# Attention plus MLP on one core: a step's block transposition moved ahead of the burst in program order, and the last turned exponential one step sooner

## The chip, the cores and the metric

The kernel runs on one core of one Trainium2 chip. The core has five engines that run their own instruction streams in order and meet through semaphores: TensorE (PE; its weight loads are shown as PEld), VectorE (DVE), ScalarE (ACT), GpSimd (POOL) and SyncE (SP, which here only issues DMAs). The metric is the device time of one execution in microseconds; lower is better.

## What is computed

An input of 2048 rows by 448 columns is normalised, and then runs through two branches whose results are added to the input: attention with 16 query heads of width 28 that share one key and one value head, and an MLP with 1792 hidden columns.

```python
xn = layernorm(x)
# branch A: 16 query heads, one key head, one value head, Dh = 28
q = (xn @ wq) as 16 heads;  k = xn @ wk;  v = xn @ wv
p = softmax(q k^T * Dh**-0.5);  A = (p v, heads side by side) @ wo
# branch B
h = gelu(layernorm(xn) @ w1 + b1);  B = h @ w2 + b2
out = x + A + B
```

## The kernel before

The first part of the kernel (to about 487 us of the span) projects q, k and v and runs the whole MLP. The rest is attention, which the change touches.

**Units and steps.** Attention is cut into 16 units `u`: four chunks of 512 query rows times four groups of four heads. A unit is worked off in 8 steps, each of two key tiles `kt`, `kt+1` of 128 keys: 128 steps `n`, step `n` being unit `n // 8`. "Position" below means `n % 8`, so `kt` = 2 x position.

**Ordinary heads.** For a pair of (key tile, head) jobs, `scores` takes a tile `p`, issues two matmuls into a PSUM tile `s` (L791) and one exponential on ACT (L793) that writes `p`, keys on partitions and queries along the free dimension. In the last eleven steps the third job of a step goes through two banks of the small PSUM pool `m` with two exponentials instead (L785, L786).

**Turned heads.** In units 2 to 15 the fourth head of the group goes another way, so that the row maximum is found on the way. `turned_scores` computes its scores with queries on partitions, four matmuls for 128 queries (L742), each evacuated by a DVE instruction that also gives a maximum (L743); these are the "t" pieces. `turned_exp` (the "x" piece) exponentiates half of such a tile on ACT (L760) and issues 8 DMAs, 5 on SP and 3 on POOL (L764), that lay it out in the tile `turned[u]` so that 32 x 32 blocks are all that is left to transpose. `turn_blocks` (the "T" piece) takes a tile `p` and transposes two key tiles' blocks from `turned[u]` into it with one DVE instruction (L769). A unit's turned scores and exponentials are made during the unit before it; its last exponential is issued at the last step of that unit, and its first transposition at its own first step, `kt` = 0.

**The burst.** The "P" piece pops two key tiles from a queue that lags by one step: the burst of step `n` multiplies with the values what step `n-1` produced, 8 multiplications for the accumulator `po` (L722; each leaves two records in the trace). Of each four, the first three read ordinary heads and the fourth reads the tile that T wrote.

**Other pieces.** "m" is one step of the stream that finds the row maxima of ordinary heads ahead of time (matmul L485, DVE reduction L486); it runs in most steps once or twice. "e" brings the maxima of the next unit into place, once a unit (L468 to L473). "o" is one output tile (12 matmuls L636 to L638, one DVE addition L640), when there is one. "n" moves the normalisation of the finished unit on (among others the reciprocal L666 on DVE, small DMAs and products on POOL). At `kt` = 0 `load_q` loads the queries of the next unit (L457, tile `xh`, issued on POOL).

**Order.** Nothing is scheduled: each engine runs its instructions in the order in which the Python program emits them. A string gives that order for a step, one letter a piece; for turned units it is the second one of

```python
ORDERS = ("mptmpmtmpmexnPpmonm", "ptmpeoxnPptmTn")
```

so a turned step is: p, t, m, p, e, o, x, n, burst, p, t, m, T, n. `jobs` starts with three jobs, one taken by each "p".

**Buffers.** Tiles `p` come from a ring of 7, four taken per step. `turned` has two tiles, `raw` (scores of the turned head) three. The PSUM pool `m` has three banks, shared by t, m, e, o and, at the end, the third p; `s` has two double banks and `po` one bank.

Of the kernel before, what the change touches and what calls it, by code (L numbers as in the profile page):

```python
# [24 lines left out]
SCALE = DH ** -0.5  # L25
BURST = 2
MLP_MAX = 20
ORDERS = ("mptmpmtmpmexnPpmonm", "ptmpeoxnPptmTn")
TURNED = tuple(range(2, 16))
RAWS = 3  # L30
LEAD = 11
# [5 lines left out]
def block_kernel(ctx, tc, x, wq, wk, wv, wo, w1, b1, w2, b2, out):  # L37
# [361 lines left out]
    NU = len(units)  # L399
# [16 lines left out]
    for c in range(NCH):  # L416
        center, turn = norm_parts((c + 1) % NCH, c + 1 == NCH)
        for i in range(4):
# [7 lines left out]
            if i in ((2, 3) if c == 0 else (1, 3)):  # L426
                n = 2 * c + i // 3
# [19 lines left out]
    def load_q(u):  # L447
        c, g = units[u]
        cols = slice(c * CW, (c + 1) * CW)
        if u < 2:  # L450
            qst.append(xt_p.tile([P, 4, CW], F32R, name="xh"))
            pool.memset(f(qst[u]), 0.0)
        qs = qst[u % 2]
        for blk, i in ((1, 0), (2, 0), (0, 1), (3, 1)):
            nh = heads_of(u)
            src = qd[i][4 * DH * g:4 * DH * g + DH * nh, cols].rearrange("(j r) n -> r j n", r=DH)
            loads.dma_start(f(qs[32 * blk:32 * blk + DH, 0:nh, :]), src)  # L457
        qss[u] = qs
# [5 lines left out]
    def load_max(u):  # L464
        qs, mr = qss[u], mrs.pop(u)
        nh = heads_of(u)
        pm = mtile([nh * CT, P])
        pe.transpose(pm, mr[:, 0:nh * CT], ident)  # L468
        mn = keep.tile([4 * CT, 2, P], F32R, name="mn", bufs=1)[0:nh * CT]
        act.activation(mn[:, 0, :], pm, AF.Copy, scale=-1.0)  # L470
        dve.scalar_tensor_tensor(mn[:, 1, :], pm, -1.0, f(mn[:, 0, :]), op0=ALU.mult, op1=ALU.subtract)
        loads.dma_start(f(qs[60:61, 0:nh, :]), f(mn[:, 0, :]))
        loads.dma_start(f(qs[124:125, 0:nh, :]), f(mn[:, 1, :]))  # L473
# [128 lines left out]
    def turned_tile():  # L602
        return att.tile([P, 4 * CT, CW], F32, name="turned", bufs=2)
# [14 lines left out]
    def prep_wo(g):  # L618
        act.activation(woh[:, g, :], wor[:, g, :], AF.Copy)
        pool.tensor_sub(wol[:, g, :], wor[:, g, :], f(woh[:, g, :]))  # L620
# [8 lines left out]
    def o_jobs(c, gs, tiles=range(CT)):  # L629
        last = NG - 1 in gs  # L630
        for k in tiles:
            po = mtile([P, D])
            ts = slice(k * P, (k + 1) * P)
            for g in gs:
                oth, otl = ots[c, g]
                pe.matmul(po, oth[:, ts], woh[:, g, :], start=(g == gs[0]), stop=False)  # L636
                pe.matmul(po, oth[:, ts], wol[:, g, :], start=False, stop=False)  # L637
                pe.matmul(po, otl[:, ts], woh[:, g, :], start=False, stop=(g == gs[-1]))  # L638
            a = rows[c, k]
            dve.tensor_add(a, a, po)  # L640
            if last:
                (nc.scalar if k % 2 and c == NCH - 1 else nc.sync).dma_start(ov[:, CT * c + k, :], a)
            yield
# [73 lines left out]
    def pv(u, kt):  # L717
        if kt == 0:
            pos[u] = op.tile([P, CW], F32, name="po")
        po = pos[u]  # L720
        for j in range(4):
            pe.matmul(po[32 * j:32 * j + 32, :], vs[:, kt, :], ps.pop((u, kt, j)),  # L722
                      start=(kt == 0), stop=(kt == NT - 1))
        if kt == NT - 1:
            if u == NU - 1:
                end_jobs(u, pos.pop(u))
                return
            side.add(norm_jobs(u, pos.pop(u)))
            side.step()
            c, g = units[u]  # L730
            if c < NCH - 1 and g == NG - 1:
                oside.add(o_wait(c, range(NG), range(CT)))
# [20 lines left out]
    def turned_exp():  # L753
        if not exps:
            return
        u, t, raw, m3, h = exps.pop(0)
        if u not in turned:
            turned[u] = turned_tile()
        rs = slice(2 * h, 2 * h + 2)
        act.activation(raw[:, rs], raw[:, rs], AF.Exp, bias=m3[:, 4:5], scale=1.0)  # L760
        for r in range(2 * h, 2 * h + 2):
            for a in range(4):
                q = pool if a == 3 or (a == 2 and r % 2) else nc.sync
                q.dma_start(turned[u][32 * r:32 * r + 32, 4 * t + a, :],  # L764
                            raw[32 * a:32 * a + 32, r].rearrange("p b i -> p (b i)"))

    def turn_blocks(u, kt):
        p = pair_of()
        dve.transpose(p.rearrange("p k (g j) -> p g k j", j=32),  # L769
                      turned[u][:, :, 32 * kt:32 * kt + 64].rearrange("p g (k j) -> p g k j", j=32))  # L770
        ps[u, kt, 3], ps[u, kt + 1, 3] = p[:, 0], p[:, 1]
# [8 lines left out]
    def scores(u, kt, jobs, apart):  # L780
        p = pair_of()
        if apart:
            for i, (k, j) in enumerate(jobs):
                s = mtile([P, CW])
                pe.matmul(s, ks[:, (kt + k) * P:(kt + k + 1) * P], qss[u][:, j, :], start=True, stop=True)  # L785
                act.activation(p[:, i], s, AF.Exp, scale=SCALE)  # L786
                ps[u, kt + k, j] = p[:, i]
            return
        s = sp.tile([P, 2, CW], F32, name="s")
        for i, (k, j) in enumerate(jobs):  # L790
            pe.matmul(s[:, i], ks[:, (kt + k) * P:(kt + k + 1) * P], qss[u][:, j, :], start=True, stop=True)  # L791
            ps[u, kt + k, j] = p[:, i]
        act.activation(p, s, AF.Exp, scale=SCALE)  # L793
# [12 lines left out]
    for n, (u, kt) in enumerate(steps):  # L806
        if n == 8:
            loads = pool
        if 4 <= n < 4 + NG:
            prep_wo(n - 4)  # L810
        if u + 1 < NU and kt == 0:
            load_q(u + 1)
        jobs = [((0, 0), (0, 1)), ((0, 2), (1, 2)), ((1, 0), (1, 1))]
        if u not in TURNED:
            jobs[1:2] = [((0, 2), (0, 3)), ((1, 2), (1, 3))]
        for what in ORDERS[u in TURNED]:
            if what == "p":
                scores(u, kt, jobs.pop(0), n >= len(steps) - LEAD and len(jobs) == 0)
            elif what == "m":
                if maxed < total - left + left * sum(weight[:n + 1]) / sum(weight):  # L820
                    maxed += mxs.step()
            elif what == "t":
                if n >= 8 * (TURNED[0] - 1) - 2:
                    tq.step()
            elif what == "x":
                turned_exp()
            elif what == "T":
                if u in TURNED:
                    turn_blocks(u, kt)
            elif what == "e":  # L830
                if kt == (6 if u + 2 < NU else 10) and u + 1 < NU:
                    load_max(u + 1)
            elif what == "n":
                side.step()
            elif what == "o":
                if n == len(steps) - 5:
                    oside.add(o_jobs(NCH - 1, range(NG - 1)))
                oside.step()
            elif what == "P":
                for _ in range(BURST if n else 0):  # L840
                    pv(*pvq.pop(0))
# [29 lines left out]
```

## Time and profile before

| | us |
|---|---|
| median of 3 runs | 1194.95 (1194.28 to 1195.69) |
| profiled execution | 1195.62 |
| its span, first to last instruction | 1193.9 |
| attention of turned units, of the span | 582 to 1182 |
| busy in 582 to 1133 (551.0 long): PE, DVE, ACT, POOL | 546.0, 360.9, 411.7, 317.9 |

The granted TensorE clock is 1.00 throughout. "Busy" counts an instruction from its start to its end; on PE the ends are modelled. A wait is written as "who <- whom: total us, times, longest". In a timeline a line is: start, length, engine, line of the program, operation, tiles as out<-in, and in square brackets the idle time before and what ended it; "x16" means that 16 instructions in a row are merged. DMAs have a line at the engine that issues them (SPq, POOL), and in the chain of waits a piece "DMA" for the time to their landing.

### The profile page before, as it was taken

The numbers are of one execution on the slowest core, as the hardware profiler recorded it, in microseconds if no ns is written. First come the engines' busy times: TensorE is split into PE (matmuls) and PEld (weight loads), VectorE is DVE, ScalarE is ACT, GpSimd is POOL, SyncE is SP. The second block draws the span as 40 slices with busy tenths as digits, with TensorE's granted clock in tenths as the row PEclk, the third lists the DMA queues.
The fourth block names the chain that finished last, engine by engine and source line by source line (L and its number), as shares of the span: only waits on it lengthen the run. The fifth ranks groups of instructions, "written<-read, shape, count | busy, mean of one in ns | idle before, by whom it ended". The sixth has DMA issues, their size and how long they took to land.

```text
span 1193.9 us, 17703 instructions
## 1 busy us (share of the span) xinstructions
PE 1175.4 (98%) x5793; PEld 725.9 (61%) x5793; DVE 896.0 (75%) x1676; ACT 667.4 (56%) x789; POOL 505.1 (42%) x779
## 2 busy tenths in 40 slices
PE   9999999999999999999999999999999999999998
PEld 8778888888888888644444445344445444454444
DVE  7799999999999999877667665666665666666634
ACT  5842321221221112578777775777775877776773
POOL 5333331131113123135565664475655476554530
PEclk9999999999999999999999999999999999999999
DMA  8751101001000110314445654554654554653520
GB/s 274 217 162 55 31 24 47 24 16 54 16 24 16 55 47 25 90 37 126 117 134 130 166 142 126 129 143 126 163 150 118 135 148 118 164 144 105 139 55 31
DMA packets 72489, 120.06 MB, mean 101 GB/s; under 512 B 24678, under 2 KB 33572, under 8 KB 72396
## 3 DMA queue, kind: packets, MB, share of 16 engines
q1 hardware_dynamic: 49484, 74.75, 22.1%
q0 software_dynamic: 21504, 43.59, 14.5%
q8 instruction: 46, 0.75, 0.3%
q10 hardware_dynamic: 1408, 0.57, 0.2%
q14 instruction: 47, 0.39, 0.1%
HBM read 45.19 MB, written 13.88 MB: 49 GB/s over the span
## 4 chain that ended last, share of the span: by engine, by line
PE 86%; DVE 7%; DMA 2%; ACT 2%; issue 1%; SPq 0%; POOL 0%; DVEq 0%; ACTq 0%; POOLq 0%
PE po L722 24%; PE s L791 16%; PE m L485 15%; PE ph L169 9%; PE m L742 4%; PE m L542 4%; PE m L544 4%; PE m L540 4%; DVE mx L486 2%; DMA xh<-qd 1%; PE m L636 1%; PE ph L172 1%; PE ph L174 1%; PE m L638 1%; PE m L637 1%
## 5 line engine op out<-in xcount | busy, mean ns | idle before, releaser
L486 DVE TENSOR_REDUCE mx<-m 128x1 f32<-128x512 f32 x800 | 526.6, 688 | 49.1 <-PE m L485 43.5
L793 ACT ACTIVATE p<-s 128x1024 f32<-128x1024 f32 x389 | 382.2, 1026 | 159.3 <-PE s L791 158.5
L485 PE MATMUL m<-ks,qm 128*128 128x512 f32 x800 | 321.6, 405 | 1.3 <-DVE mx L486 0.6
L722 PE MATMUL po<-p,vs 128*32 128x512 f32 x2048 | 314.0, 600 | 2.7 <-DVE p L769 2.7
L743 DVE TENSOR_SCALAR_CACHE_REDUCE raw<-m 128x512 f32<-128x512 f32 x224 | 150.5, 672 | 177.6 <-PE m L742 175.4
L791 PE MATMUL s<-xh,ks 128*128 128x512 f32 x778 | 260.9, 419 | 1.7 <-ACT p L793 0.8
L764 POOL DMA_DIRECT2D turned<-raw x336 | 168.8, 508 | 162.2 <-ACT raw L760 155.1
L791 PEld LDWEIGHTS s<-xh,ks 128*128 128x128 f32 x778 | 131.8, 188 | 140.3 <-ACT raw L760 68.8
L526 ACT ACTIVATE hr<-ph,b1t 128x512 f32<-128x512 f32 x56 | 38.5, 688 | 305.5 <-PE ph L174 281.7
L531 POOL TENSOR_TENSOR hl<-hr,hh 128x512 fp32r<-128x512 f32 x56 | 72.2, 1290 | 301.6 <-PE m L485 284.5
L485 PEld LDWEIGHTS m<-ks,qm 128*128 128x128 f32 x800 | 150.2, 188 | 52.8 <-DVE raw L743 16.7
L722 PEld LDWEIGHTS po<-p,vs 128*32 128x32 f32 x2048 | 68.2, 108 | 177.0 <-issue 116.2
L769 DVE STREAM_TRANSPOSE p<-turned 128x1024 f32<-128x1024 f32 x112 | 138.5, 1237 | 18.0 <-PE po L722 9.4
L760 ACT ACTIVATE raw<-raw,m 128x1024 f32<-128x1024 f32 x112 | 127.5, 1139 | 0.0
L742 PE MATMUL m<-ks,q 128*128 128x512 f32 x224 | 88.5, 395 | 0.0
L540 PE MATMUL m<-w2h,hh 128*128 128x448 f32 x224 | 82.4, 368 | 0.0
L544 PE MATMUL m<-w2h,hl 128*128 128x448 f32 x224 | 82.0, 366 | 0.0
L542 PE MATMUL m<-w2l,hh 128*128 128x448 f32 x224 | 81.9, 366 | 0.0
L169 PE MATMUL ph<-xh,w1l 128*128 128x512 f32 x168 | 66.3, 394 | 0.0
L169 PE MATMUL ph<-xl,w1h 128*128 128x512 f32 x168 | 66.1, 393 | 0.0
L169 PE MATMUL ph<-xh,w1h 128*128 128x512 f32 x168 | 66.1, 393 | 0.0
L742 PEld LDWEIGHTS m<-ks,q 128*128 128x128 f32 x224 | 42.1, 188 | 10.6 <-DVE raw L743 0.6
(153 smaller groups left out, 1129.4 us busy)
## 6 DMA issues: line engine op xcount, KB each, us to landing
turned<-raw SPq DMA_DIRECT2D x560, 64.0 KB
turned<-raw POOLq DMA_DIRECT2D x336, 64.0 KB, 2.3
xh<-qd POOLq DMA_DIRECT2D x56, 168.0 KB, 4.7
qm<-qd SPq DMA_DIRECT2D x160, 56.0 KB
qd<-qe SPq DMA_DIRECT2D x24, 256.0 KB
tr<-ld POOLq DMA_DIRECT2D x56, 64.0 KB, 2.6
raw<-in_B_w_dram SPq DMA_DIRECT2D x7, 448.0 KB
acc<-in_A_x_dram SPq DMA_DIRECT2D x3, 896.0 KB
```

The source lines that it names most:

```text
L169: pe.matmul(ps, w, v, start=(n == 0), stop=False)
L485: pe.matmul(pm, qm[:, t * P:(t + 1) * P], ks[:, n * CW:(n + 1) * CW], start=True, stop=True)
L486: dve.tensor_reduce(mx[:, CT * j + t, n:n + 1], pm, axis=AX.X, op=ALU.max)
L540: pe.matmul(m2[k], hh[:, ts], w2h[:, ft, :], start=(ft == 0), stop=False)
L544: pe.matmul(m2[k], hl[:, ts], w2h[:, ft, :], start=False, stop=(ft == NF - 1))
L722: pe.matmul(po[32 * j:32 * j + 32, :], vs[:, kt, :], ps.pop((u, kt, j)), start=(kt == 0), stop=(kt == NT - 1))
L742: pe.matmul(sc, q3[i][:, t * P:(t + 1) * P], ks[:, n * CW:(n + 1) * CW], start=True, stop=True)
L743: dve.tensor_scalar(raw[:, :, 4 * n:4 * n + 4, :].rearrange("p r b i -> p b r i"), sc.rearrange("p (b r i) -> p b r i", r=4, i=32), SCALE, ...
L764: q.dma_start(turned[u][32 * r:32 * r + 32, 4 * t + a, :], raw[32 * a:32 * a + 32, r].rearrange("p b i -> p (b i)"))
L769: dve.transpose(p.rearrange("p k (g j) -> p g k j", j=32), turned[u][:, :, 32 * kt:32 * kt + 64].rearrange("p g (k j) -> p g k j", j=32))
L791: pe.matmul(s[:, i], ks[:, (kt + k) * P:(kt + k + 1) * P], qss[u][:, j, :], start=True, stop=True)
L793: act.activation(p, s, AF.Exp, scale=SCALE)
```

## The change

Two edits. First, the order string of turned units has a second T behind the second p, and each T runs only if its condition holds: `jobs` still holds a job at the first place and is empty at the second, so that at `kt` = 0 the transposition is emitted at the old place, and at all other steps (7 of 8) at the new one, ahead of e, o, x, n and the burst. Second, at step 8 * 15 - 2 = 118, `turned_exp` is called twice, so that both halves of the last turned tile of unit 15 are exponentiated in step 118 and none is left for step 119.

```diff
-ORDERS = ("mptmpmtmpmexnPpmonm", "ptmpeoxnPptmTn")
+ORDERS = ("mptmpmtmpmexnPpmonm", "ptmpTeoxnPptmTn")
...
             elif what == "x":
                 turned_exp()
+                if n == 8 * (NU - 1) - 2:
+                    turned_exp()
             elif what == "T":
-                if u in TURNED:
+                if u in TURNED and (kt == 0) == (not jobs):
                     turn_blocks(u, kt)
```

## The prediction

> **Which number to start from.** The profiled execution took 1195.62 us, its span is 1193.9 (1.7 lie around it); the median of the runs shown is 1194.95 (1194.28 to 1195.69). The sum below is made in the span and subtracted from the median. Two runs of this kernel differ by up to 0.12%, so I call anything within 0.2% (2.4 us) no change.
>
> **What bounds the kernel.** First the page: TensorE looks full.
>
> ```profile
> PE 1175.4 (98%) x5793; PEld 725.9 (61%) x5793; DVE 896.0 (75%) x1676; ACT 667.4 (56%) x789; POOL 505.1 (42%) x779
> PE 86%; DVE 7%; DMA 2%; ACT 2%; issue 1%; SPq 0%; POOL 0%; DVEq 0%; ACTq 0%; POOLq 0%
> ```
>
> Taken at its word, 98% leaves 18.5 us in the whole span, and in the stage of the turned units (582 to 1133 us, PE 546.0 busy of 551.0) only 5. But a matmul's end is modelled, so a matmul that sits in the queue waiting for its operand counts as busy. The table of waits shows it, on the weight loads, which precede the matmuls:
>
> ```profile
> PEld po L722 <- DVE p L769: 58.0, 88, 2.4
> ...
> PEld m L636 <- DVE raw L743: 4.8, 3, 1.8
> ```
>
> Eighty-eight times TensorE waits for the block transposition (L769) inside the burst (L722); three times an output tile (L636) waits for a DVE evacuation (L743), of which more below. The timeline of two neighbouring steps shows the length of it:
>
> ```profile
> 912.42 1.92 PE L722 MATMUL po<-p,vs 128*32 128x512 f32 x16
> ...
> 915.28 0.69 DVE L743 TENSOR_SCALAR_CACHE_REDUCE raw<-m 128x512 f32<-128x512 f32 x1 [2.13 <-PE m L742]
> ...
> 915.89 0.69 DVE L486 TENSOR_REDUCE mx<-m 128x1 f32<-128x512 f32 x1
> ...
> 916.50 1.24 DVE L769 STREAM_TRANSPOSE p<-turned 128x1024 f32<-128x1024 f32 x1
> 916.93 2.76 PE L722 MATMUL po<-p,vs 128*32 128x512 f32 x16
> ...
> 917.78 0.16 PEld L722 LDWEIGHTS po<-p,vs 128*32 128x32 f32 x8 [0.71 <-DVE p L769]
> ...
> 917.96 1.14 ACT L760 ACTIVATE raw<-raw,m 128x1024 f32<-128x1024 f32 x1
> ```
>
> The same 16 records take 1.92 us at 912.42 and 2.76 at 916.93. The second burst issues three multiplications, then the fourth (head 3) waits until the transposition issued at 916.50 ends at 917.74. So there is a loop over two engines: burst ends, then (about 0.95 us later, L791 and L742) DVE evacuates the second "t" (0.69) and "m" (0.69), transposes (1.24), and only then can the next burst go on. ScalarE is not the loop: three exponentials (3.01 merged) and the turned one (1.14) are 4.15 us per step.
>
> I measured all bursts this way, from the timeline's L722 rows: start to start is the period, length above 1.92 the stall. Period minus stall is nearly one number: median 4.50 us over the 48 steps without an output tile that have two maxima ("m"), 4.36 over the 40 with one. That is the stall-free pace, and it already contains every other wait. The stalls, summed over steps 17 to 117 by position in the unit (step mod 8; the burst at position 0 multiplies the previous unit's last rows):
>
> position: 0 10.1, 1 10.0, 2 8.5, 3 5.2, 4 8.0, 5 8.1, 6 9.6, 7 7.4; together 66.9 us.
>
> **Part 1, T ahead of the burst.** No instruction is added or removed. The transposition of step n (112 of 1.24) goes from behind the second t and m of its step to behind the first m. It is read by the burst of step n+1.
> - *Its cost in the new place.* DVE's order becomes t, m, T, t, m. With S the start of a burst: the first t and m end near S + 0.9 (two maxima), T near S + 2.2; the next t is ready at S + 1.85 + 1.0 = 2.85. So T lies under the burst with some 0.6 to spare, and DVE's sum is 2 x 0.67 + 2 x 0.69 + 1.24 = 4.0 of 4.36 to 4.50. Cost 0; if this cover were gone, the next t would be late by up to 1.24, and with it the maximum behind it and the PSUM bank that "m" needs.
> - *Its tile.* Seven tiles "p", four taken per step: the one it takes was last read by the burst of step n-1, long done. The third "p" now takes the slot that burst n reads first; its score matmuls stand behind that burst anyway. Cost 0.
> - *Queued behind it on DVE:* L471 (once a unit, 0.27), L666, L640 (0.62). The first feeds row loads needed four steps later; the adds free a bank wanted four allocations later. Cost 0.
> - *What it removes, positions 2 to 6:* 8.5 + 5.2 + 8.0 + 8.1 + 9.6 = **39.5 us**.
> - *Positions 7, 0 and 1 are another matter,* since at kt = 0 T stays where it was. Its rows come from the exponential one step before, through 8 DMAs. The chain at a unit's start:
>
> ```profile
> 661.01 1.15 ACT raw L760
> 662.43 0.87 POOL turned L764 x2
> ...
> 663.91 1.26 POOL xh L457 x2
> 665.17 4.99 DMA xh<-qd
> 670.19 1.25 DVE p L769
> 671.49 1.90 PE po L722 x10
> ```
>
> From the exponential's end (662.15) to T 8.0 us pass; where T had an idle gap before it (units 3, 4, 5, 6, 8, 10, 14) the same distance is 7.9, 8.0, 8.0, 8.2, 7.9, 8.3, 7.5. From the start of burst 8u-1 to the end of burst 8u+1 that makes 2.16 + 7.9 + 1.24 + 1.94 = 13.2 us; measured 12.8 to 13.7. The faster pace would want 4.43 + 4.43 + 1.92 = 10.8. So the stalls at positions 7 and 0 do not vanish, they gather at position 1: about 2.4 us there instead of 0.8. I book nothing for units 3, 4, 6, 8, 10, 14, and 0.2 to 0.3 each (**0.7**) for 7, 11, 12, whose T found its rows landed. Lower bound of the landing 5.25 us (unit 15), upper 8.3. Units 5, 9 and 13 have output tiles there (2.6 us more PE work in the step), which covers the landing: they gain both stalls, 0.85 + 0.57 + 0.38 + 1.03 + 0.85 + 0.57 = **4.2**. Unit 2 keeps its 0.92 at step 17.
>  A released wait at the very moment that xh<-qd lands (670.16, T 670.19) is odd, as T doesn't read xh. The Trainium skill, "DMA: Bandwidth & Descriptors", section "Queues, rings and completion order", says that a DMA's semaphore write lands only after every earlier write of that DMA engine, across its queues; by that the 168 KB of xh loads, which the faster pace does not move relative to the exponential, hold T as before. If only the turned rows' own bytes counted, the third rival's time would hold.
> - *Output tiles.* At steps 42, 74 and 106 the first t stood behind T and kept the bank of the output matmul (1.37 us at 727.64): periods 8.69, 8.09, 8.69 against 7.04, 6.80, 7.04. With T behind t this goes, but for some 0.3 each that the reciprocal and t still take: **3.7**.
>
> **Part 2, two exponentials in step 118.** 8 DMAs and one ACTIVATE move one step ahead, past step 118's last exponentials and 119's. SP then issues ten in a row (0.63 each), POOL six.
>
> ```profile
> 1148.43 1.06 PE L722 MATMUL po<-p,vs 128*32 128x512 f32 x6
> ...
> 1149.68 1.25 DVE L769 STREAM_TRANSPOSE p<-turned 128x1024 f32<-128x1024 f32 x1 [5.73 <-ACT p L793]
> ```
>
> Here burst 121 waits 2.5 us. Steps 118 on need no t and m: their pace is 3.45, and ScalarE (4.2 with a turned exponential) is level with it. From S(117) = 1132.89: burst 118 loses its 1.25 (part 1), so S(118) = 1136.57; x runs 1138.1 to 1139.25 and 1140.3; step 118's last exponentials end 1141.4, costing burst 119 about 0.3. SP's last issue starts 5.6 after 1139.25, landing 2.5 later (as at 1147.21 to 1149.68): T at 1147.35, ended 1148.6, burst 121 ends 1150.5 instead of 1152.87. 2.3, less the 0.3 already in position 5: **2.0**. Without part 2 the same working gives 1151.6, so it is worth about 1. Bounds: 0 (SP queue late by 2) to 3. The final burst's 0.15 (length 2.07) goes too.
>
> **Sum:** 39.5 + 0.7 + 4.2 + 3.7 + 2.0 + 0.15 = 50.3 us; 1194.95 - 50.3 = **1144.6**. Its own range, with a mean landing between 7.4 and 8.4 (9 units x 0.5 = 4.5) and 2 us for the rest: 1138 to 1152.
>
> **Rivals.**
> 1. *A slower engine sets the pace.* ScalarE is busy 4.15 of 4.36. If its order stretches the freed steps (56 of them) to 4.7 on average, 0.27 x 56 = 15 comes back: 1160. For it: the little slack. Against: 4.36 and 4.50 came out of steps where ScalarE did the same work.
> 2. *Unit starts get worse.* POOL waits in order for ld<-rc (29.4 us in 13 waits); closer steps could push the rows' DMAs later. 1.5 us more at nine starts: 1158.
> 3. *Unit starts get better,* landing near unit 15's 5.25: the start costs 11.6 instead of 13.2, 9 x 1.6 = 14 more: 1130. Against it: only unit 15 has no xh loads behind its rows.
> 4. *TensorE is the bound after all,* and only the stage's 5 us of idle PE can be had: 1190. The Trainium skill, "Trainium Kernel Development and Optimization", section "Performance Expectations", calls matmul busy time a bad metric since matmuls are pipelined; the 1.92 against 2.95 for equal bursts says the same.
> 5. *Slower:* the landing at the unit starts grows until it eats all. Nine starts pay in full, three have 0.45 spare: 9a + 3(a - 0.45) = 50.3 gives a = 4.3 us from which it decides; at 5 it costs 58.7: 1203. For it: SP is in order (3.1 us of issues in a 4.4 us step) and POOL too. Against: seven landings within 0.8 us of each other.
> 6. *No effect:* T still comes late, because its slot is freed only in the burst that should follow it: 1195. Against: the count of slots above.
>
> **Chances.** Forecast 0.66; rival 1 0.10; 2 0.06; 3 0.08; 4 0.04; 5 0.04; 6 0.02. Faster 0.66 + 0.10 + 0.06 + 0.08 + 0.04 = 0.94, same 0.02, slower 0.04. The range from 1133 to 1163 holds the forecast and rivals 1 and 2, and leaves 0.18 out.
>
> **What would show it.** PEld L722 waiting for L769 falls from 58 us in 88 waits to about 13 waits at step 8u+1 of 1 to 3 us each; bursts at positions 2 to 7 are 1.92 long; periods 4.36 and 4.50; T begins right after the first m. x-end to T at unit starts stays 7.5 to 8.3. Wrong if bursts are 1.92 but periods stay near 5 (another loop), if DVE's t waits behind T, or if burst 8u+1 stalls over 4 us.

## The result, and the profile after

| | before | after |
|---|---|---|
| median, us | 1195.32 (4 runs, 1194.28 to 1198.93) | 1147.8 (4 runs, 1144.9 to 1148.63) |
| ratio | | 0.9593 [0.9567, 0.9619] |
| profiled execution, us | 1195.62 | 1147.51 |
| its span, us | 1193.9 | 1145.7 |

The kernel became 4% faster, 3.2 us short of the forecast of 1144.6. The page after, with the shares of the engines and of the chain that ended last:

```profile
PE 1123.2 (98%) x5793; PEld 715.9 (62%) x5793; DVE 900.4 (79%) x1676; ACT 663.3 (58%) x789; POOL 505.1 (44%) x779
PE 83%; DVE 6%; DMA 4%; ACT 3%; issue 2%; POOL 2%; SPq 1%; DVEq 0%; ACTq 0%; POOLq 0%
```

TensorE is as "busy" as before, 98%, with the same 5793 instructions, although 52 us of that busy time are gone. So the share said nothing about the room that was there. DMA's part of the chain doubled from 2% to 4%: that is what now ends last at the units' starts. The table of waits (who waits for whom: total, times, longest) tells it on the same rows as before, where the first had 58.0 us in 88 waits and the last 4.8 in 3:

```profile
PEld po L722 <- DVE p L769: 21.0, 13, 3.2
...
DVE p L769 <- DMA xh<-qd: 10.3, 6, 2.6
...
DVE p L769 <- DMA turned<-raw: 6.5, 3, 3.1
...
PEld m L636 <- DVE raw L743: 1.3, 2, 0.6
```

Thirteen waits are left, and the transposition now waits in its turn for DMAs that land (which one the profile names is not always right, see below). The timeline of two neighbouring steps (step 77, then step 78):

```profile
889.12 0.68 DVE L743 TENSOR_SCALAR_CACHE_REDUCE raw<-m 128x512 f32<-128x512 f32 x1
889.56 1.92 PE L722 MATMUL po<-p,vs 128*32 128x512 f32 x16
...
889.73 0.69 DVE L486 TENSOR_REDUCE mx<-m 128x1 f32<-128x512 f32 x1
890.33 1.24 DVE L769 STREAM_TRANSPOSE p<-turned 128x1024 f32<-128x1024 f32 x1
890.59 1.14 ACT L760 ACTIVATE raw<-raw,m 128x1024 f32<-128x1024 f32 x1
892.42 0.69 DVE L743 TENSOR_SCALAR_CACHE_REDUCE raw<-m 128x512 f32<-128x512 f32 x1 [0.85 <-PE m L742]
...
893.99 1.92 PE L722 MATMUL po<-p,vs 128*32 128x512 f32 x16
```

The transposition runs behind the maximum (L486) and under the burst, is over at 891.57, and DVE still idles 0.85 us before the next t has its scores. Over all transpositions of steps 17 to 117 the median of that idle time is 0.66 us. Both bursts are 1.92 long.

What is left stands at the starts of the units. The chain of waits around the start of unit 6 (start, length, what):

```profile
741.98 1.90 PE po L722 x16
743.87 0.03 ACTq L652
743.90 0.18 ACT raw L760
744.08 0.28 issue
744.37 4.00 DMA turned<-raw
748.37 1.24 DVE p L769
749.60 0.04 issue
749.64 1.90 PE po L722 x10
```

Burst 48 ends; burst 49 can end only when the turned rows have landed and the one transposition that kept its old place is done. The DMA that the chain names is not the one waited for: it was issued at 744.37 with rows of the next unit, and by the semaphore counts in the trace it landed at 749.24, after the transposition had begun. The profile gives no landing for DMAs issued by SP. By the same counts the last of unit 6's row DMAs on SP, issued at 742.71, landed at 747.93, 0.42 us before the transposition (748.35). In 10 of the 12 starts of units 3 to 14 the transposition begins 0.41 to 0.57 us after that landing, whatever DMA the profile names; in units 7 and 11 the rows on POOL, issued late, land last. The stalls (burst length above 1.92) in steps 17 to 117, by position in the unit, us:

| position | 0 | 1 | 2 to 6 | 7 | together |
|---|---|---|---|---|---|
| before | 10.1 | 10.0 | 39.5 | 7.4 | 66.9 |
| after | 0.0 | 21.4 | 0.2 | 0.0 | 21.7 |

So 45.2 us of stalls went, and two thirds of the 17.5 that positions 7 and 0 lost came back at position 1. The stall-free paces are 4.50 us with two maxima, as before, and 4.42 with one, where 4.36 stood: 2.3 us lost over some 36 steps.

### The profile page after: what moved, and what is told of

Same layout as the page of the kernel before. It is cut to its first block, busy times and chain, and to the rows that moved or that the text cites. A ratio compares the mean times of both kernels' runs of the same rounds, so it can differ in the third digit from the quotient of the medians.

```text
span 1145.7 us, 17740 instructions
## 1 busy us (share of the span) xinstructions
PE 1123.2 (98%) x5793; PEld 715.9 (62%) x5793; DVE 900.4 (79%) x1676; ACT 663.3 (58%) x789; POOL 505.1 (44%) x779
## 4 chain that ended last, share of the span: by engine, by line
PE 83%; DVE 6%; DMA 4%; ACT 3%; issue 2%; POOL 2%; SPq 1%; DVEq 0%; ACTq 0%; POOLq 0%
PE po L722 18%; PE s L791 15%; PE m L485 15%; PE ph L169 9%; PE m L544 4%; PE m L542 4%; PE m L540 4%; PE m L742 3%; DVE mx L486 2%; ACT p L793 2%; DMA xh<-qd 2%; DMA turned<-raw 2%; PE qp L169 1%; PE m L636 1%; PE ph L172 1%
## 5 line engine op out<-in xcount | busy, mean ns | idle before, releaser
L486 DVE TENSOR_REDUCE mx<-m 128x1 f32<-128x512 f32 x800 | 526.7, 688 | 49.0 <-PE m L485 43.5
L793 ACT ACTIVATE p<-s 128x1024 f32<-128x1024 f32 x389 | 379.5, 1026 | 125.7 <-PE s L791 125.2
L722 PE MATMUL po<-p,vs 128*32 128x512 f32 x2048 | 260.0, 599 | 9.6 <-DVE p L769 9.5
L743 DVE TENSOR_SCALAR_CACHE_REDUCE raw<-m 128x512 f32<-128x512 f32 x224 | 153.3, 684 | 116.1 <-PE m L742 102.9
L722 PEld LDWEIGHTS po<-p,vs 128*32 128x32 f32 x2048 | 55.1, 109 | 143.0 <-issue 118.3
```

The source lines that it names most:

```text
L486: dve.tensor_reduce(mx[:, CT * j + t, n:n + 1], pm, axis=AX.X, op=ALU.max)
L743: dve.tensor_scalar(raw[:, :, 4 * n:4 * n + 4, :].rearrange("p r b i -> p b r i"), sc.rearrange("p (b r i) -> p b r i", r=4, i=32), SCALE, ...
```

## The experiments

Ratios are to the kernel before, with a 95% interval; the kernel after has 0.9593 [0.9567, 0.9619]. Stalls are those of the table above.

**Each part alone.** First without the second edit, then without the first:

```diff
                 turned_exp()
-                if n == 8 * (NU - 1) - 2:
-                    turned_exp()
```

> The changed kernel without the second exponential at step 118. My theory: the order of the transposition does nearly everything. Against the kernel before, ratio about 0.960 to 0.961 (some 1147 to 1149 us); step 118's burst stays free, the exponential of step 119 comes back and burst 121 waits some 1 us longer than in the changed kernel (stall near 2.5 instead of 1.4), burst 119 loses its stall of 0.5. Rival (part 2 carries a good share): more than 4 us slower than the changed kernel.

Measured: 1148.08 us, 0.9602 [0.9581, 0.9622]. Burst 121 stalls 2.44 us (1.40 in the kernel after), and burst 119 not at all (0.47).

```diff
-ORDERS = ("mptmpmtmpmexnPpmonm", "ptmpTeoxnPptmTn")
+ORDERS = ("mptmpmtmpmexnPpmonm", "ptmpeoxnPptmTn")
...
-                if u in TURNED and (kt == 0) == (not jobs):
+                if u in TURNED:
```

> The kernel before with only the second exponential at step 118. My theory: 1 to 1.5 us faster than before at most (ratio 0.999), all of it at burst 121; the stalls at positions 0 to 7 stay at 67 us in sum and the weight loads of the burst still wait some 56 us for the transposition. Rival: the same share as in the changed kernel's total, ratio 0.99 or lower.

Measured: 1194.96 us, 0.9993 [0.9984, 1.0002], no change that can be told. Its row in the table of waits:

```profile
PEld po L722 <- DVE p L769: 55.9, 86, 2.0
```

Nearly all 88 waits are back, and the stalls sum to 66.8. Within what two runs differ by, the whole gain is the first part. From the start of burst 117 to the end of burst 121 the four kernels take 19.98 us (before), 18.34 (second part alone), 18.39 (first part alone), 17.82 (both): the second part is worth 1.64 us in the old order and 0.57 in the new one, where the rows' own landing ends last. In the kernel after and in the one without the second edit the first transposition of unit 15 reads:

```profile
1101.47 1.25 DVE L769 STREAM_TRANSPOSE p<-turned 128x1024 f32<-128x1024 f32 x1 [7.70 <-PE s L791]
```

```profile
1104.82 1.25 DVE L769 STREAM_TRANSPOSE p<-turned 128x1024 f32<-128x1024 f32 x1 [8.27 <-DMA turned<-raw]
```

It is the same wait in both: by the semaphore counts SP's last row DMA landed 0.42 us before the transposition in each (at 1101.05 and at 1104.40). The first line names TensorE, which this transposition has nothing to read from. The releaser is the last event before the start by the profile and not always the cause.

**Where in the step.** The transposition ahead of the first t instead of behind the first m, and behind the burst's piece instead of ahead of it:

```diff
-ORDERS = (..., "ptmpTeoxnPptmTn")
+ORDERS = (..., "pTtmpeoxnPptmTn")
```

> The changed kernel with the transposition (except at kt = 0) still one piece earlier, ahead of the step's first t and m. On VectorE its neighbours are then those of the kernel before: second t, second m, transposition, first t. What differs from before is that it belongs to the step that follows, so that a whole burst lies between it and its reader. Theory A (what was removed is the loop from the second t and m through the transposition to the very next burst): stalls at positions 2 to 7 stay at zero; the first t stands behind the transposition again, which only costs the waits of the output tiles (periods 8.7 and 8.1 at three steps, 3.3 us): 1148 to 1153 us, ratio 0.961 to 0.965. Theory B (the neighbours on VectorE matter: first t and m late behind the transposition set the pace): paces of 4.9 us and more, ratio over 0.975.

Measured: 1151.35 us, 0.9639 [0.9619, 0.9658]. No stalls outside position 1 (21.9 there), the same paces, but steps 42, 74 and 106 take 8.71, 8.08 and 8.70 us again, where the kernel after has 7.57, 6.98 and 7.56: 3.4 us. The first t behind the transposition holds the bank of the output tile, as the prediction read it from before.

```diff
-ORDERS = (..., "ptmpTeoxnPptmTn")
+ORDERS = (..., "ptmpeoxnPTptmTn")
```

> The changed kernel with the transposition (except at kt = 0) emitted behind the burst, but ahead of the step's second t and m. Theory A (it must come ahead of the second t and m, the burst itself is immaterial, since on VectorE only e, o and n lie between): within 3 us of the changed kernel, ratio 0.957 to 0.962, stalls at positions 2 to 7 zero. Theory B (it must stand ahead of the burst): the stalls come back, ratio over 0.98.

Measured: 1145.13 us, 0.9589 [0.9575, 0.9603], no stalls outside position 1 (19.1 there). The place relative to the burst in program order decides nothing; the place ahead of the second t and m on DVE does. TensorE meets the burst in its own queue either way.

**Is the cover real?** At every moved transposition half of it is done a second time, 98 times 0.62 us more work on DVE; the result is unchanged.

```diff
+        if kt:
+            dve.transpose(p[:, 0].rearrange("p (g j) -> p g j", j=32),
+                          turned[u][:, :, 32 * kt:32 * kt + 32])
```

> The changed kernel with half of each transposition outside kt = 0 done a second time (98 times one more VectorE instruction over 128 x 512, about 0.62 us), the result unchanged. My working gave the transposition in its new place about 0.6 us of cover, and VectorE 3.6 to 4.0 of 4.4 to 4.5 us of work per step. Theory A (that cover is real): 0 to 8 us slower than the changed kernel (1148 to 1156). Theory B (VectorE is already level with the pace): 0.62 x 80 = 50 us slower, near 1195.

Measured: 1153.4 us, 0.9657 [0.9643, 0.9671]; paces of 4.51 and 4.42, position 1 at 23.3, the others at nothing. Of 61 us of added work 5.6 show in the time. The cover is there: the idle time before the next t, 0.66 us in the median, fell to nothing, and 0.62 nearly fit in it.

**What holds the start of a unit.** The loads of the next unit's queries (L457) moved from a unit's first step to its third, from unit 2 on:

```diff
-        if u + 1 < NU and kt == 0:
+        if u + 1 < NU and kt == (4 if u > 1 else 0):
             load_q(u + 1)
```

> The changed kernel with the loads of the next unit's queries issued two steps later (kt = 4 instead of 0, from unit 2 on). What is left of the stalls stands at the first burst after a unit's start, 21 us in 13 units, and the transposition there is released when the query loads land. Theory A (those loads hold the landing of the turned rows): from the exponential's end to the transposition 5.3 to 6.5 us instead of 6.2 to 9.0, the stalls there fall to 8 to 12 us, the kernel is 9 to 13 us faster than the changed one (about 1135, ratio 0.950). Theory B (the issue of eight DMAs on two queues and their own landing make up the time): distances and stalls as in the changed kernel, within 2 us of it.

Measured: 1134.76 us (1134.26 to 1134.81), 0.9491 [0.9475, 0.9506]: 13.0 us faster than the kernel after. The stalls at position 1 fall from 21.4 to 8.4. The same start of unit 6 in the timeline of the kernel after, and below it in this one:

```profile
738.44 1.14 ACT L760 ACTIVATE raw<-raw,m 128x1024 f32<-128x1024 f32 x1
739.87 1.48 POOL L764 DMA_DIRECT2D turned<-raw  x3 [1.85 <-ACT raw L760]
741.34 2.39 POOL L457 DMA_DIRECT2D xh<-qd  x4
...
748.35 1.25 DVE L769 STREAM_TRANSPOSE p<-turned 128x1024 f32<-128x1024 f32 x1 [2.89 <-DMA turned<-raw]
...
749.64 0.16 PEld L722 LDWEIGHTS po<-p,vs 128*32 128x32 f32 x8 [3.23 <-DVE p L769]
```

```profile
734.95 1.14 ACT L760 ACTIVATE raw<-raw,m 128x1024 f32<-128x1024 f32 x1
...
736.38 1.47 POOL L764 DMA_DIRECT2D turned<-raw  x3 [1.86 <-ACT raw L760]
...
741.97 1.25 DVE L769 STREAM_TRANSPOSE p<-turned 128x1024 f32<-128x1024 f32 x1
...
743.27 0.14 PEld L722 LDWEIGHTS po<-p,vs 128*32 128x32 f32 x5 [0.31 <-DVE p L769]
```

From the exponential's end to the transposition 8.8 us became 5.9, and TensorE's wait 3.23 became 0.31; over units 3 to 14 the mean went from 7.65 to 6.55 (5.9 to 8.2, wider than the 5.3 to 6.5 expected). The landing is what became shorter: SP's last row DMA was issued 2.6 us after the exponential's end in the one kernel and 2.5 in the other (means of these units), but from issue to landing, by the semaphore counts, it took 4.4 us (2.8 to 6.1) before the move and 2.7 (2.0 to 4.2) after it. So the query loads (four a unit, 168 KB each, against 64 KB for each of the rows' DMAs), issued on POOL while the rows were on their way, held the rows back. The rule that the prediction drew from the Trainium skill, "DMA: Bandwidth & Descriptors", section "Queues, rings and completion order" (the semaphore's write waits for every earlier write of that DMA engine), fits this; that the loads only share the DMA engines' time with the rows would fit it as well, and no run here tells the two apart.

The other way to the same end leaves the loads and makes the rows of every unit a step earlier, as the second edit does for unit 15:

```diff
-                if n == 8 * (NU - 1) - 2:
+                if n % 8 == 6:
                     turned_exp()
```

> The changed kernel with both halves of the last turned tile exponentiated in the step before the last one in every unit (position 6), not in unit 15's lead alone. My theory: at unit starts only the landing counts, so one step of lead (4.4 us, less some 3 that SP spends on ten issues in a row) takes away most of the 21 us of stalls at position 1: down to 8 to 12. ScalarE then has 5.3 us of work in that step and gives back 0.5 to 1 us in each of 13 units: net 3 to 10 us faster than the changed kernel (1138 to 1145). Rival (ScalarE sets the pace there): the loss of 1 us or more in each unit eats it all, no faster than the changed kernel.

Measured: 1139.05 us, 0.9529 [0.9515, 0.9544]. Position 1 falls to 7.9, as with later loads, but the step with two turned exponentials is 0.33 to 0.41 longer in each unit. Both at once:

```diff
-        if u + 1 < NU and kt == 0:
+        if u + 1 < NU and kt == (4 if u > 1 else 0):
...
-                if n == 8 * (NU - 1) - 2:
+                if n % 8 == 6:
```

> The changed kernel with both edits for the unit starts: query loads two steps later, and both halves of the last turned tile one step sooner in every unit. If the two only shorten the same wait, what is left at position 1 is the loop through the late transposition at kt = 0 (0.4 to 0.9 us a unit, 8 us in sum, as each edit alone left it), and the kernel is no faster than the better one, 1134 to 1139. If each still left landing time uncovered, 3 to 6 us faster: 1129 to 1132.

Measured: 1138.14 us, 0.9527 [0.9511, 0.9543], position 1 at 7.0. The two shorten the same wait: together they take 1.3 us more off position 1 than later loads alone, and the longer steps cost more than that.

**The rest at position 1.** With the rows that early, the first transposition of a unit could also go ahead (on top of the last kernel):

```diff
-                if u in TURNED and (kt == 0) == (not jobs):
+                if u in TURNED and (u == TURNED[0] and kt == 0) == (not jobs):
```

> The kernel with both edits for the unit starts, and the transposition ahead of the burst at kt = 0 too (but in unit 2). With rows exponentiated a step sooner they land about when the early transposition wants to start, so that the last 7 us of stalls at position 1 (the loop at kt = 0) go: about 1131 to 1133, ratio 0.947. Rival (the rows land later than that, and VectorE, in order, holds t and m behind the waiting transposition): the stall moves to VectorE, no faster than 1137.

Measured: 1145.98 us, 0.9586 [0.9564, 0.9609], a miss. The stalls are gone (1.0 left, unit 2's), but steps 40, 72 and 104 take 10.46, 12.13 and 11.52 us instead of 6.9. In the table of waits of this kernel, and in its timeline around step 72:

```profile
DVE p L769 <- DMA turned<-raw: 15.6, 8, 4.9
```

```profile
858.89 1.25 DVE L769 STREAM_TRANSPOSE p<-turned 128x1024 f32<-128x1024 f32 x1 [4.95 <-DMA turned<-raw]
...
860.06 0.65 DVE L743 TENSOR_SCALAR_CACHE_REDUCE raw<-m 128x512 f32<-128x512 f32 x1
...
860.88 0.71 PE L636 MATMUL m<-woh,oth 128*128 128x448 f32 x1 [3.60 <-DVE raw L743]
```

DVE stands 4.95 us in the transposition's wait; behind it are the t pieces that free the banks which the output tile needs, and TensorE idles 3.60 us for one of them. At this start the rows came late because POOL issued their last six DMAs only from 853.80 on, 7.15 us after the exponential's end at 846.65, behind two instructions of the normalisation (L680, L681) and four loads of q (L409). Not all of the 13.4 us that the three steps lost is waiting: some 5 are a slower TensorE clock behind each wait (last section). The next attempt put it between the second t and the second m, with later loads alone:

```diff
-ORDERS = (..., "ptmpTeoxnPptmTn")
+ORDERS = (..., "ptmpTeoxnPptTmn")
```

> The changed kernel with the query loads two steps later, and the late transposition at kt = 0 between the second t and m instead of behind both. If the loop through t, m and the transposition is what is left at position 1 (8.4 us, of which 0.69 us per unit with two maxima is the m), it loses 2 to 5 us: 1130 to 1133. Rival (by then the rows have just landed, so that it waits for them anyway and m waits behind it): within 1.5 us of the kernel with the query loads later (1134.8).

Measured: 1139.08 us, 0.9537 [0.9511, 0.9564], a miss by the same mechanism: position 1 at 6.9, but steps 40 and 104 at 9.06 and 11.55, the maximum (L486) now being what waits behind it, as the output tile of step 104 shows:

```profile
1012.96 0.45 PE L636 MATMUL m<-woh,oth 128*128 128x448 f32 x1 [2.87 <-DVE mx L486]
```

**The pace of 4.42.** Suspected was the ring of 7 tiles "p": with the new order the third exponential of a step gets a tile that the burst of the same step reads, where in the old order it got one that the burst of the step before had read. An eighth tile, on top of later loads (one tile less of "oth" and "otl" makes the room):

```diff
-        return att.tile([P, 2, CW], F32, name="p", bufs=2 * BURST + 3)
+        return att.tile([P, 2, CW], F32, name="p", bufs=2 * BURST + 4)
...
-        ots[c, g] = [att.tile([P, CW], F32R, name=n, bufs=5) for n in ("oth", "otl")]
+        ots[c, g] = [att.tile([P, CW], F32R, name=n, bufs=4) for n in ("oth", "otl")]
```

> The changed kernel with the query loads two steps later, and a ring of eight tiles p instead of seven (room for it comes from one buffer less of each of the two normalised tiles, five to four). In the changed kernel a step with one maximum takes 4.42 us instead of 4.36: the third exponential takes the slot of the first one of the step before, and has a semaphore instruction of its own ahead of it. With eight tiles every piece meets its own slot of two steps before. Theory: the pace falls back to 4.36, 2 to 3 us less than with seven tiles (1132 to 1133). Rival (the 0.06 comes from VectorE or the PSUM banks): the pace stays 4.42 and the time within 1 us of 1134.8.

Measured: 1132.49 us (1132.04 to 1132.76), 0.9476 [0.9462, 0.9490], 2.3 us below the kernel with later loads. The pace is back at 4.36 to 4.37, position 1 at 9.1. The ring was the cause: the other half of the edit only takes tiles away (it was not run alone), and with seven tiles, too, steps with one maximum keep 4.36 at position 0, where the order is the old one. By which path is not settled: the semaphore instructions that ACT executes ahead of L793 rose from 209 to 248 with the change, which fitted an extra wait, but with eight tiles there are 271 of them and the pace is right.

On top of it, once more the transposition between t and m at a unit's start, but not in units 5, 9 and 13, where output tiles follow:

```diff
-ORDERS = (..., "ptmpTeoxnPptmTn")
+ORDERS = (..., "ptmpTeoxnPptTmTn")
...
-        for what in ORDERS[u in TURNED]:
+        for at, what in enumerate(ORDERS[u in TURNED]):
+            last = at == 14
...
-                if u in TURNED and (kt == 0) == (not jobs):
+                if u in TURNED and (kt == 0) == (not jobs) and (u, kt, 3) not in ps and (
+                        kt > 0 or u % 4 != 1 or last):
```

> The kernel with later query loads and eight tiles, and the late transposition between the second t and m at kt = 0, but not in units 5, 9 and 13, which have output tiles at their start. In the run with it everywhere the bursts' stalls at position 1 fell from 8.4 to 6.9 us, but steps 40 and 104 grew to 9.1 and 11.6 us (6.9 before): the m behind the waiting transposition held a PSUM bank that the output tile needs. Theory: without those units 1 to 2 us faster than with eight tiles alone, 1130 to 1131.5, steps 40, 72 and 104 at 6.8 to 6.95. Rival (other steps paid as well): 1133 or more.

Measured: 1131.98 us (1130.58 to 1135.26), 0.9485 [0.9467, 0.9504]. Steps 40, 72 and 104 stay at 6.93, 6.79 and 6.93 and position 1 falls to 7.2, both as expected, but in the time it can't be told from the kernel with eight tiles. That one, later loads and eight tiles, is the best that is settled: 15.3 us below the kernel after.

## Why the prediction was right, step by step

| term | predicted | measured |
|---|---|---|
| positions 2 to 6 | 39.5 | 39.2 |
| starts of units without output tiles | 0.7 | 3.9 |
| starts of units 5, 9, 13 | 4.2 | 2.1 |
| banks of output tiles | 3.7 | 3.4 |
| last unit | 2.0 | 1.9 |
| last burst | 0.15 | -0.06 |
| pace with one maximum | 0 | -2.3 |
| sum | 50.3 | 48.1 |

The spans differ by 48.2. The forecast lies 3.2 below the median: 2.1 of it are in the sum, 0.7 in medians that differ by only 47.5, and 0.4 in a median before that is higher than the one the forecast started from.

- *The loop over two engines was the bound.* Four fifths of the gain are its term, within 0.3. TensorE as the bound (rival 4) is out: its busy time fell with its work unchanged. So is rival 6, a transposition that comes late anyway.
- *The cover* held at the predicted place; the idle time left was 0.66 us in the median where 0.6 was worked out, and the doubled half transposition filled it. ScalarE as the pace (rival 1) is out: steps with two maxima kept 4.50.
- *The gathering at position 1* was read rightly from the chain: positions 7 and 0 gave up 17.5 us and position 1 took 11.4 more. The step "about 2.4 us there" was rough: the nine units lie between 0.74 and 3.36. The distance from the exponential's end to T, said to stay at 7.5 to 8.3, went from 6.2 to 9.0. The mean fell from 7.85 to 7.65, and the starts without output tiles gained 3.9 in place of 0.7. The wait that the prediction found odd was not one for xh: the last row DMA on SP landed at 669.62 by the semaphore counts, 0.57 us before the T at 670.19. The query loads made that landing late, but it is the rows that T waits for.
- *Units 5 and 9 failed:* the step "output tiles there cover the landing" took 8.0 us from exponential to transposition; it was 9.0 in both, and bursts 41 and 73 stall 1.1 each. In unit 13 it was 6.4, and the stall is nothing. This size and that of the other starts went wrong in opposite directions; that they nearly cancel, together with the lost pace, is luck.
- *Rivals 2 and 5* (starts worse) did not come about on the mean. Rival 3 (starts better) was put aside because query loads stand behind the rows of every unit but the last; that reason was right, for the run that took them away gave 1134.8, near that rival's 1130.
- *Its tile, "cost 0",* failed as a size: the new slot of the third "p" costs nothing in steps with two maxima, but 0.06 us in those with one, 2.3 in sum, and an eighth tile took it back.
- *Part 2* was put at 1 us by the working without it; on top of the first part it showed 0.57. The landing behind SP's ten issues came out as worked: burst 117 to the end of burst 121 took 17.82 against 17.6.

## What to carry to other kernels

A TensorE that is busy for 98% can still wait: the rows of its weight loads, and the length of equal bursts, show for what. If the operand of step n+1 is already there in step n, its preparation belongs ahead of the work on the same engine that comes due later; but an instruction that may wait for a DMA does not belong ahead of the evacuations that free PSUM banks (13 us lost in three steps here, some 5 of them by the clock that fell behind the waits). When such a loop is gone, ask which transfers were issued next to the ones that now end last: moving loads that nobody needed yet gave another 13 us for one line.

## What the runs showed of the hardware

TensorE's clock fell after a short idle time. In the kernel with the transposition between t and m, TensorE idled 2.87 us before the output matmul at 1012.96; the windows around it (window, length, busy time with counts of PE, PEld, DVE, ACT and POOL, granted clock, DMA share, GB/s):

```profile
1005.00:1013.60 8.60, 5.73 (x31) 2.88 (x31) 4.61 (x10) 7.03 (x8) 7.15 (x15) 1.00 0.59 169
1013.60:1017.00 3.40, 3.40 (x11) 2.54 (x9) 1.58 (x2) 0.00 (x0) 2.75 (x5) 0.53 0.64 165
1017.00:1025.00 8.00, 7.98 (x50) 4.65 (x53) 4.49 (x9) 3.91 (x4) 1.02 (x2) 0.99 0.39 110
```

For 3.4 us the granted clock was 0.53, and the output matmuls followed each other every 0.37 us, against 0.20 in the kernel after (from its 1020.4 on). So the wait of 2.87 us cost about 1.5 more behind it: eight matmuls at 0.17 extra are 1.4, and the burst behind them took 1.99 instead of 1.92. In the kernel with every transposition ahead (but unit 2's first), each of the three long steps has such a stretch of 3.41 us at a granted clock of 0.50, from 700.15, 860.58 and 1021.01 on, around idle times of 1.85, 3.60 and 2.90 us. Half of 3 x 3.41 is 5.1 us, and the idle times sum to 8.35: together about the 13.4 us that these steps lost. The length of the idle time alone does not decide: 2.32 us in the kernel after (before 749.64) and 1.89 in the kernel with the transposition between t and m (before 698.05) were followed by a granted clock of 1.00. What else decides is not shown here. The Trainium skill, "TensorE: Matmul & The Clock Gate", section "Part 1: The HAM clock gate (the "warmup" mystery)", puts the slow clock behind at least one idle window of about 3.4 us; here shorter idle times were enough in three of four cases, and the measurement decides.
